# A retention layer with a mish feed-forward: the order of states and y in the opening, two conversions on GpSimd, and identity matmuls of 32 columns

## The chip, the core and the metric

The kernel runs on one core of a Trainium2 chip. The core has TensorE (PE in the profile; its weight loads are listed as PEld), VectorE (DVE), ScalarE (ACT), GpSimd (POOL) and SyncE (SP), which issues the loads and stores. The metric is the device time in microseconds of one execution of the program.

## The reference

Two steps. First a recurrent retention over 4 batches, 8 heads, 768 positions and a head dimension of 64; then a feed-forward layer on the 3,072 rows that come out, with 512 inputs, 2,048 hidden columns and the activation mish, h · tanh(softplus(h)).

```python
for t in range(S):
    state = gamma[None, :, None, None] * state + np.einsum('bhd,bhe->bhde', k[:, :, t], v[:, :, t])
    y[:, :, t] = scale * np.einsum('bhd,bhde->bhe', q[:, :, t], state)
...
h = x @ w_in
sp = np.where(h > 20.0, h, np.log1p(np.exp(np.minimum(h, 20.0))))
g = h * np.tanh(sp)
return (g @ w_out).astype(np.float32)
```

## The kernel before

The recurrence is computed in chunks of 128 positions, six to a batch, 24 in all. For a chunk, TensorE forms the *scores* k·q, VectorE multiplies them by a mask (and converts them to 16 bits), TensorE multiplies the masked scores with v (the *present* part of y) and the incoming state with q (the *past* part). The *outer* products of k and v, summed over the chunk, renew the state. The powers of gamma are put into q, k and v when they are converted from 32 to 16 bits, so that a state only has to be multiplied once every two chunks (by the table gch).

The work is cut into blocks: the first has four chunks, ten more have two. For each block the kernel forms y, turned so that it can be the input of the feed-forward (tile xt), then h = x·w_in with mish (tile g), then g·w_out. Later blocks replace eight block products by seven, with sums of quarter matrices (wsum, gsum, tmat) made on VectorE. All instructions are written in the order in which each engine runs them; every engine takes its own in that order, and the waits between engines follow from the tiles. PSUM tiles come from pools of a few banks (mmps with 3, atps with 2, pxps with 1); a new tile waits until the readers of the one that had its bank before are done.

The change lies nearly all in `first_block`, the opening. It treats the first four chunks as two *pairs*, 0 and 1. The steps, with the lines that the profile names:

- `load_first_q`, `load_pair` (L254, L298): SyncE loads q of the first four chunks, then k of both pairs in halves, then v of both pairs in halves, then the weights of the first matrix in pieces (L200, tile wi).
- `cast_first_q`, `cast_pair` (L279, L315, L319): conversion of q on VectorE, of pair 0's k on VectorE, of pair 1's k on GpSimd, of all four halves of v on ScalarE (L315: a plain multiplication by a constant).
- `spin` (L477): matmuls of the identity into a scratch bank whose result nobody reads.
- `turn_first_q`, `turn_pair` (L266, then a copy on ScalarE, L270): turning q and k on TensorE by a matmul with the identity.
- `pair_scores` (L349 and the mask on VectorE, L357, which writes am for pair 0 and a part of wsum for pair 1), called for each half of each pair.
- `pair_outer` (L370), into u; `pair_state` (L381 to L388) makes from it, in turn, the states named mid (after the first chunk of a pair: a copy on ScalarE for pair 0, an addition on VectorE for pair 1) and sth (after the second chunk: on VectorE an addition into suh and a multiplication).
- `pair_present` (L398) in two halves of 16 matmuls, the second marked own; `pair_past` (L408), 8 matmuls; both add up in y for pair 0 and in z for pair 1. Between the two halves of present a tiny copy named seen reads one column of y (ScalarE, L1350) or of z (VectorE, L1357); the second half waits for it.
- `pair_xt` (L425): ScalarE copies y and z into xt. The first h matmuls, `open_in` (L699), read xt and the weights that `cast_win` (L224) converts on GpSimd and VectorE; `next_in` (L727) and `g1` (L744) go on with h, one *unit* of 128 hidden columns after another.

GpSimd also writes the mask tables: keep_four, tri_half and keep_two. Only keep_four is used in the opening.

`IN_HALVES` names units of h whose matmuls of 512 columns are written as two of 256.

Of the kernel before, what the change touches and what calls it, by code (L numbers as in the profile page):

```python
# [12 lines left out]
ALU = mybir.AluOpType  # L13
# [3 lines left out]
def kernel(  # L17
# [91 lines left out]
    for h in range(H):  # L109
        p0 = h // 2 % 2 * D  # L110
        nc.gpsimd.memset(
            gch[p0:p0 + D, h // 4 * 2 + h % 2], float(gamma[h] ** (2 * C)))
    seen = cpool.tile([P, 1], FP32, name="seen")
# [14 lines left out]
    IN_HALVES = {0: range(NFB - 7, NFB), 1: range(NFB - 4, NFB), 2: range(NFB)}  # L128
# [171 lines left out]
    def cast_pair(n, nm, a, scales=None, on=None):  # L300
# [13 lines left out]
        if scales is None:  # L314
            nc.scalar.mul(dst, src, BOOST)  # L315
        else:
            by = scale_by_head(scales[:, mine]) if nm != "v" else scales[:, mine].unsqueeze(
                3).broadcast_to((P, H // 2, 2, D))
            (on or nc.gpsimd).tensor_tensor(dst, src, by, op=ALU.mult)  # L319
# [151 lines left out]
    def spin(n, per=HP, to=None):  # L471
        if to is None:
            to = pairs[min(x for x in pairs if type(x) is tuple and x[1] == "at")]
            to = to.rearrange("p h i r c -> p h (i r) c")
        for i in range(0, n, per):
            m = min(per, n - i)
            nc.tensor.matmul(  # L477
                to[:, 0, :m], ident, ident.unsqueeze(1).broadcast_to((P, m, P)),
                start=True, stop=True)

# [10 lines left out]
    def half(n):  # L491
        return slice(n * D, (n + 1) * D)
# [797 lines left out]
    def first_block():  # L1290
# [17 lines left out]
        nc.gpsimd.memset(tri_half, 0.0)  # L1308
        for n in range(2):
            nc.gpsimd.affine_select(  # L1310
                out=tri_half[half(n)], in_=tri_half[half(n)], compare_op=ALU.is_gt, fill=1.0,
                base=0, pattern=[[-1, 2], [-2, D // 2]], channel_multiplier=1)
        keep_from(keep_two, 2, [[1, 2], [-1, 2], [-2, D]])
        spin(38, 1)
        spin(2, 2)
# [12 lines left out]
        spin(8)  # L1328
        pair_scores(0, 1)
        turn_pair(1, "k", 0, True)  # L1330
        cast_pair(0, "v", 0)
        turn_pair(1, "k", 1, True)
        cast_pair(0, "v", 1)
        cast_pair(1, "v", 0)
        pair_at(1, 0)
# [13 lines left out]
        spin(6, to=aside)  # L1349
        nc.scalar.copy(seen, y[1][:, 1, 0, :1])  # L1350
        cast_pair(1, "v", 1)
        pair_present(0, y, True)
        pair_past(0, y, 1)
        pair_state(0, u, 1)
# [3 lines left out]
        u = u_next  # L1358
        for a in range(2):
            pair_outer(1, u, a)  # L1360
        for m in range(2):
            pair_xt(0, y, m)
        pair_state(1, u, 0)
# [276 lines left out]
```

## Time and profile before

| | |
|---|---|
| median of 3 runs | 190.93 us (190.66 to 191.94) |
| the profiled execution | 190.69 us |
| its span in the trace | 188.9 us |
| TensorE busy | 183.6 us (97%) |
| VectorE, ScalarE, GpSimd busy | 142.9, 111.5, 65.3 us |
| mean granted TensorE clock | 1.0 of full speed |

The span runs from the program's first instruction to its last; the execution's own time is 1.8 us longer. Times in the rows are counted from the start of the span. A busy TensorE in a row means that matmuls follow one another without a gap; the end of a matmul is modelled and includes its way through the array, so that neighbours overlap in the rows and the distance of their starts is what one costs.

### The profile page before, as it was taken

The page shows a single profiled execution, that of the slowest core. Times are in us where ns is not written, and L with a number is a line of the kernel's source. Part 1 is how long each engine was busy: PE and PEld are TensorE (multiplying, and loading weights), DVE is VectorE, ACT ScalarE, POOL GpSimd, SP SyncE. Part 2 cuts the span into 40 slices and gives each one's busy share as a digit, 9 for nine tenths or more (in the row PEclk, how much of TensorE's full clock was granted, in tenths as well). Part 3 has the DMA queues.
Part 4 walks back from the last instruction along what each step waited for, and adds up shares of the span by engine and source line. Part 5 has one row for each costly group of instructions (what it writes and reads, how often), then busy time and mean ns, then how long its engine had stood idle before and what let it go on. Part 6 is the DMA issues. An engine that isn't in the chain of part 4 may idle for free.

```text
span 188.9 us, 7938 instructions
## 1 busy us (share of the span) xinstructions
PE 183.6 (97%) x3438; PEld 163.6 (87%) x3438; DVE 142.9 (76%) x310; ACT 111.5 (59%) x213; POOL 65.3 (35%) x93
## 2 busy tenths in 40 slices
PE   7999999999999999999999999999999999999993
PEld 7756478888898998998998998998998998988983
DVE  0888679885977967887898597687698698666862
ACT  3575767264646554793684584683673773874651
POOL 5072000578509246331354614714534800000000
PEclk9999999999999999999999999999999999999999
DMA  5999999999999899999999886993999980301103
GB/s 166 308 312 388 386 385 367 298 325 219 192 240 307 177 209 238 208 205 233 214 197 261 209 169 148 188 225 85 220 173 240 218 162 5 115 3 51 64 0 116
DMA packets 83235, 38.84 MB, mean 206 GB/s; under 512 B 58240, under 2 KB 76288, under 8 KB 83200
## 3 DMA queue, kind: packets, MB, share of 16 engines
q1 hardware_dynamic: 82912, 38.22, 85.8%
q8 instruction: 27, 0.44, 1.0%
q10 hardware_dynamic: 288, 0.11, 0.2%
q14 instruction: 8, 0.07, 0.1%
HBM read 27.31 MB, written 6.29 MB: 178 GB/s over the span
## 4 chain that ended last, share of the span: by engine, by line
PE 92%; DMA 3%; SPq 1%; POOL 1%; issue 1%; ACT 0%; DVE 0%; POOLq 0%; DVEq 0%
PE h_ps L957 27%; PE o_ps L1179 23%; PE h_ps L744 12%; PE o_ps L1073 10%; PE o_ps L801 7%; DMA kf<-in_k_dram 3%; PE y_ps L620 3%; PE h_ps L699 2%; PE u_ps L514 1%; PE at L506 1%; PE y_ps L398 1%; POOL qk L319 1%; PE h_ps L727 1%; PE t_ps L266 1%; PE at L349 1%
## 5 line engine op out<-in xcount | busy, mean ns | idle before, releaser
L957 PE MATMUL h_ps<-xt,wsum 128*128 128x128 f16 x512 | 33.5, 219 | 0.0
L969 ACT ACTIVATE g<-h_ps 128x512 f16<-128x512 f32 x48 | 27.5, 598 | 6.6 <-PE h_ps L957 6.6
L957 PEld LDWEIGHTS <-wsum 128*128 128x128 f16 x512 | 29.9, 98 | 0.0
L957 PE MATMUL h_ps<-xt,win 128*128 128x128 f16 x384 | 28.0, 219 | 0.0
L957 PEld LDWEIGHTS <-win 128*128 128x128 f16 x384 | 23.6, 98 | 0.3
L1179 PEld LDWEIGHTS <-gsum 128*128 128x128 f16 x232 | 21.5, 98 | 2.6
L744 PE MATMUL h_ps<-xt,win 128*128 128x128 f16 (+2 forms) x276 | 23.7, 246 | 0.0
L744 PEld LDWEIGHTS <-win 128*128 128x128 f16 x276 | 20.4, 98 | 3.0
L753 ACT ACTIVATE g<-h_ps 128x512 f16<-128x512 f32 x26 | 15.5, 597 | 10.2 <-PE h_ps L744 10.2
L1179 PE MATMUL o_ps<-tmat,gsum 128*128 128x256 f16 (+1 forms) x176 | 21.5, 268 | 0.0
L458 POOL TENSOR_TENSOR v<-vf,qvs 128x512 f16<-128x512 f32 x18 | 18.9, 1067 | 6.1 <-DMA vf<-in_v_dram 6.1
L439 POOL TENSOR_TENSOR qk<-qf,qvs 128x512 f16<-128x512 f32 x18 | 18.7, 1041 | 1.3 <-PE y_ps L398 1.3
L1021 DVE TENSOR_TENSOR h_ps<-h_ps,hsum 128x512 f32<-128x512 f32 x16 | 11.1, 695 | 10.2 <-PE h_ps L957 10.1
L1179 PEld LDWEIGHTS <-g 128*128 128x128 f16 x184 | 16.5, 98 | 1.6
L1000 ACT COPY h_ps<-h_ps 128x512 f32<-128x512 f32 x16 | 9.3, 584 | 12.6 <-issue 8.7
L678 ACT CAST xt<-y_ps 128x512 f16<-128x512 f32 x16 | 10.8, 738 | 8.6 <-PE y_ps L620 8.6
L1189 ACT COPY snap<-o_ps 128x256 f32<-128x256 f32 (+1 forms) x22 | 8.2, 373 | 11.0 <-PE o_ps L1179 11.0
L1179 PE MATMUL o_ps<-wout,g 128*128 128x256 f16 (+1 forms) x120 | 14.5, 265 | 0.0
L453 POOL TENSOR_TENSOR qk<-kf,qvs 128x512 f16<-128x512 f32 x12 | 12.5, 1043 | 4.6 <-DMA kf<-in_k_dram 4.6
L1538 POOL COPY summed<-gsum 128x1 f16<-128x1 f16 x7 | 1.6, 234 | 36.1 <-DVE gsum L918 28.7
L801 PEld LDWEIGHTS <-g 128*128 128x128 f16 x120 | 11.4, 98 | 1.7 <-DVE tmat L895 0.2
L1202 DVE TENSOR_TENSOR osb<-o_ps,snap 128x256 f32<-128x256 f32 (+1 forms) x22 | 9.1, 414 | 4.3 <-ACT snap L1189 2.8
(128 smaller groups left out, 343.9 us busy)
## 6 DMA issues: line engine op xcount, KB each, us to landing
out_dram<-osb SPq DMA_DIRECT2D x22, 256.0 KB, 4.0
qf<-in_q_dram SPq DMA_DIRECT2D x18, 256.0 KB, 5.0
kf<-in_k_dram SPq DMA_DIRECT2D x14, 256.0 KB, 5.6
vf<-in_v_dram SPq DMA_DIRECT2D x14, 256.0 KB, 5.5
wt<-in_moe_w_out_dram SPq DMA_DIRECT2D x6, 512.0 KB, 8.7
vf<-in_v_dram SPq DMA_DIRECT2D x20, 128.0 KB, 3.9
wi<-in_moe_w_in_dram SPq DMA_DIRECT2D x4, 512.0 KB, 8.7
kf<-in_k_dram SPq DMA_DIRECT2D x16, 128.0 KB, 4.1
```

The lines of the kernel that those rows point to most:

```text
L439: nc.gpsimd.tensor_tensor(in_place(q16.rearrange("p (w x) d -> p w x d", x=2)), by_head(qf), scale_by_head(qs_two[:, heads]), op=ALU.mult)
L453: nc.gpsimd.tensor_tensor(dst, src, boosts.rearrange("p (w y) -> p w y", y=2).unsqueeze(3).broadcast_to((P, H // 2, 2, D)), op=ALU.mult)
L458: nc.gpsimd.tensor_tensor(cast[g][2], loaded.pop(g)[2], vs[g % 2].unsqueeze(2).broadcast_to((P, H, D)), op=ALU.mult)
L678: nc.scalar.copy(dst[:, :, x], src)
L744: nc.tensor.matmul(h_ps[:, j, cols], wins[s][f // 2][:, bp, f % 2 * P:(f % 2 + 1) * P], xts[blk][:, bp, cols], start=(bp == 0 and at == 0) ...
L753: nc.scalar.activation(gt, h_ps, AF.Mish, scale=inv_boost3)
L801: nc.tensor.matmul(banks[ij][:, t], x(f)[:, t * P:(t + 1) * P], w(f), start=ij in open_banks, stop=f == fs[-1], skip_group_check=True)
L957: nc.tensor.matmul(o_ps[:, f], w(f // 2, k)[:, f % 2 * P:(f % 2 + 1) * P], x[:, k], start=begin and f == 0 and k == 0, stop=k == 1, skip_g ...
L969: nc.scalar.activation(gt[:, f:f + n, j * C:(j + 1) * C], src, AF.Mish, scale=inv_boost3)
L1021: nc.vector.tensor_tensor(pf[p], pa[p], m5[p], op=ALU.add)
L1073: nc.tensor.matmul(o_ps[:, cols], x(f), w(f)[:, cols], start=first and z == 0, stop=z == n - 1, skip_group_check=True)
L1179: nc.tensor.matmul(o_ps[:, c:c + wide], x(f), w(f)[:, c:c + wide], start=first and f == 0 and c == cols.start, stop=f == n - 1, skip_group ...
```

## The change

The states of both pairs are now made before the second half of pair 0's present and before pair 1's y. Two of the four v halves are converted on GpSimd. The tables tri_half and keep_two are written at the program's beginning. Ahead of the first turn stand 16 identity matmuls of 32 columns and 34 of 128, in place of 38 of 128 and one of 256; six later identity turns (one matmul of 512 and one of 256) are gone, and one of two 512 wide ones behind the first turn of k. Pair 1's first k turn moves ahead of pair 0's second scores. Units 9 and 10 of the first block are written whole.

```diff
+    nc.gpsimd.memset(tri_half, 0.0)
+    for n in range(2):
+        nc.gpsimd.affine_select(
+            out=tri_half[n * D:(n + 1) * D], in_=tri_half[n * D:(n + 1) * D],
+            compare_op=ALU.is_gt, fill=1.0, base=0, pattern=[[-1, 2], [-2, D // 2]],
+            channel_multiplier=1)
+    keep_from(keep_two, 2, [[1, 2], [-1, 2], [-2, D]])
     seen = cpool.tile([P, 1], FP32, name="seen")
...
-    IN_HALVES = {0: range(NFB - 7, NFB), 1: range(NFB - 4, NFB), 2: range(NFB)}
+    IN_HALVES = {0: range(NFB - 5, NFB), 1: range(NFB - 4, NFB), 2: range(NFB)}
...
-        if scales is None:
+        if scales is None and on is not None:
+            on.tensor_tensor(
+                dst, src, boosts[:, mine].unsqueeze(2).unsqueeze(3).broadcast_to(
+                    (P, H // 2, 2, D)), op=ALU.mult)
+        elif scales is None:
             nc.scalar.mul(dst, src, BOOST)
...
+    def spin_small(n):
+        to = pairs[min(x for x in pairs if type(x) is tuple and x[1] == "at")]
+        for _ in range(n):
+            nc.tensor.matmul(
+                to[:, 0, 0, 0, :D // 2], ident, ident[:, :D // 2], start=True, stop=True)
...
             cast_pair(1, "k", a, vs_two)
-        nc.gpsimd.memset(tri_half, 0.0)
-        for n in range(2):
-            nc.gpsimd.affine_select(
-                out=tri_half[half(n)], in_=tri_half[half(n)], compare_op=ALU.is_gt, fill=1.0,
-                base=0, pattern=[[-1, 2], [-2, D // 2]], channel_multiplier=1)
-        keep_from(keep_two, 2, [[1, 2], [-1, 2], [-2, D]])
-        spin(38, 1)
-        spin(2, 2)
+        spin_small(16)
+        spin(34, 1)
         turn_first_q(0, 0)
...
         turn_pair(0, "k", 1, True)
-        spin(8)
+        spin(4)
+        turn_pair(1, "k", 0, True)
         pair_scores(0, 1)
-        turn_pair(1, "k", 0, True)
         cast_pair(0, "v", 0)
         turn_pair(1, "k", 1, True)
-        cast_pair(0, "v", 1)
+        cast_pair(0, "v", 1, None, nc.gpsimd)
         cast_pair(1, "v", 0)
+        cast_pair(1, "v", 1, None, nc.gpsimd)
         pair_at(1, 0)
...
         pair_present(0, y, False)
         aside, u_next = u_banks()
-        spin(6, to=aside)
         nc.scalar.copy(seen, y[1][:, 1, 0, :1])
-        cast_pair(1, "v", 1)
+        pair_state(0, u, 1)
+        u = u_next
+        for a in range(2):
+            pair_outer(1, u, a)
+        pair_state(1, u, 0)
         pair_present(0, y, True)
-        pair_past(0, y, 1)
-        pair_state(0, u, 1)
         z = [mmps.tile([P, 2, 2, C], FP32, name="y_ps", tag="mm") for _ in range(2)]
         pair_present(1, z, False)
         nc.vector.tensor_copy(seen, z[1][:, 1, 0, :1])
-        u = u_next
-        for a in range(2):
-            pair_outer(1, u, a)
+        pair_past(0, y, 1)
         for m in range(2):
             pair_xt(0, y, m)
-        pair_state(1, u, 0)
         pair_present(1, z, True)
         for m in range(2):
             pair_past(1, z, m)
```

VectorE's order around the opening's states, before (am and wsum are the masked scores of pairs 0 and 1, suh, sth and mid the states, win the converted weights):

```order
L357 TENSOR_TENSOR wsum_385<-at,keep_four 128x1024 x2
L386 TENSOR_TENSOR suh<-u_ps,mid 128x256
L388 TENSOR_TENSOR sth<-suh,gch 128x256
L1357 COPY seen<-y_ps 128x1
L383 TENSOR_TENSOR mid<-u_ps,sth 128x256
L224 COPY win_582<-wi 128x512 x2
```

and now, at the same place:

```order
L368 TENSOR_TENSOR wsum_397<-at,keep_four 128x1024 x2
L397 TENSOR_TENSOR suh<-u_ps,mid 128x256
L399 TENSOR_TENSOR sth<-suh,gch 128x256
L394 TENSOR_TENSOR mid<-u_ps,sth 128x256
L1370 COPY seen<-y_ps 128x1
L231 COPY win_590<-wi 128x512 x2
```

The addition that makes mid of pair 1 and the tiny copy have changed places; nothing else on VectorE has.

GpSimd's order from the table gch to the first weights, before (qk_190 is pair 1's converted k):

```order
L111 MEMSET gch 64x64 x8
L319 TENSOR_TENSOR qk_190<-kf,qvs 128x2x4x64 x2
L1308 MEMSET tri_half 128x64
L1310 AFFINE_SELECT tri_half<-tri_half 64x64 x2
L102 MEMSET keep_two 128x256
L104 AFFINE_SELECT keep_two<-keep_two 64x256 x2
L224 COPY win_582<-wi 128x512 x2
```

and now (v_369 and v_373 are the second halves of v of pairs 0 and 1):

```order
L111 MEMSET gch 64x64 x8
L113 MEMSET tri_half 128x64
L115 AFFINE_SELECT tri_half<-tri_half 64x64 x2
L102 MEMSET keep_two 128x256
L104 AFFINE_SELECT keep_two<-keep_two 64x256 x2
L330 TENSOR_TENSOR qk_204<-kf,qvs 128x2x4x64 x2
L322 TENSOR_TENSOR v_369<-vf,qvs 128x4x2x64
L322 TENSOR_TENSOR v_373<-vf,qvs 128x4x2x64
L231 COPY win_590<-wi 128x512 x2
```

The tables stand ahead of the k conversions, and two v conversions behind them.

TensorE, where pair 0's first half of present ends (its last matmul has v_359), before:

```order
L398 MATMUL y_ps<-am,v_359 64x128
L477 LDWEIGHTS ident
L477 MATMUL u_ps<-ident 128x512
L477 LDWEIGHTS ident
L477 MATMUL u_ps<-ident 128x256
L398 LDWEIGHTS v_351
L398 MATMUL y_ps<-am,v_351 64x128
```

and now:

```order
L409 MATMUL y_ps<-am,v_369 64x128
L409 LDWEIGHTS v_369
L409 MATMUL y_ps<-am,v_369 64x128
L381 LDWEIGHTS qk_204
L381 MATMUL u_ps<-v_371,qk_204 64x64
```

Two identity matmuls and the own half of present stood there; now pair 1's outer products follow at once, 32 of them, ahead of that half. TensorE's list has 6,878 rows in both versions, a weight load and a matmul counted as one row each.

## The prediction

> **What bounds the kernel now.** I read the span first, then the busy time by stretches, then the chain in order of time for the opening, where nearly all of the change lies.
>
> ```profile
> span 188.9 us, 7938 instructions
> ```
>
> ```profile
> 9.00:17.00 8.00, 7.14 (x237) 4.51 (x238) 6.74 (x11) 5.86 (x14) 4.36 (x9) 1.00 1.11 338
> 17.00:185.00 168.00, 168.00 (x3111) 151.58 (x3110) 131.61 (x292) 101.62 (x194) 58.17 (x67) 1.00 0.87 200
> ```
>
> The first figure after the comma is TensorE's busy time: 7.14 of 8.00 in the opening, and from 17 us on it never stops (168.00 of 168.00). Whatever the change does before 17 us therefore arrives undiminished at the end, and nothing later can amplify it. The question is only when the first h matmul starts.
>
> ```profile
> 10.21 1.05 POOL qk L319
> ...
> 14.42 0.34 PE y_ps L398 x13
> 14.76 0.40 issue
> 15.16 0.25 PE y_ps L398 x3
> ...
> 15.85 0.17 DVE seen L1357
> ...
> 16.06 0.42 PE y_ps L398 x16
> ...
> 16.86 3.58 PE h_ps L699 x24
> 20.44 1.73 PE h_ps L727 x8
> 22.17 8.70 PE h_ps L744 x68
> ```
>
> The opening's chain, in order of time: the last k conversion on GpSimd (which waits for its load), turns, scores and y on TensorE, a stall of 0.40 us called "issue", a tiny VectorE copy ("seen") for which the last present matmuls wait, then h. The timeline has the first h matmul at 16.79:
>
> ```profile
> 16.28 0.31 PE L408 MATMUL y_ps<-qkt,sth 64*64 64x128 f16 x8
> 16.55 0.31 PE L408 MATMUL y_ps<-qkt,mid 64*64 64x128 f16 x8
> 16.79 0.72 PE L699 MATMUL h_ps<-xt,win 128*128 128x256 f16 x5
> ```
>
> VectorE, which feeds this, in the same view:
>
> ```profile
> 12.53 2.36 DVE L357 TENSOR_TENSOR wsum<-at,keep_four 128x1024 f16<-128x1024 f32 x2 [0.34 <-PE at L349]
> 14.80 0.41 DVE L386 TENSOR_TENSOR suh<-u_ps,mid 128x256 f32<-128x256 f32 x1
> 15.32 0.42 DVE L388 TENSOR_TENSOR sth<-suh,gch 128x256 f16<-128x256 f32 x1
> 15.85 0.16 DVE L1357 COPY seen<-y_ps 128x1 f32<-128x1 f32 x1
> 16.07 0.42 DVE L383 TENSOR_TENSOR mid<-u_ps,sth 128x256 f16<-128x256 f32 x1
> ```
>
> It is packed from 12.53: two masks, then state, copy, state. And the other two helpers:
>
> ```profile
> 14.12 0.65 ACT L315 ACTIVATE v<-vf 128x512 f16<-128x512 f32 x1
> 15.56 1.07 ACT L425 CAST xt<-y_ps 128x512 f16<-128x512 f32 x2 [0.79 <-PE y_ps L408]
> 16.89 1.07 ACT L425 CAST xt<-y_ps 128x512 f16<-128x512 f32 x2 [0.26 <-PE y_ps L408]
> 9.20 2.04 POOL L319 TENSOR_TENSOR qk<-kf,qvs 128x512 f16<-128x512 f32 x2 [5.55 <-DMA kf<-in_k_dram]
> 15.63 0.61 POOL L224 CAST win<-wi 128x512 f16<-128x512 f32 x1 [2.37 <-DMA wi<-in_moe_w_in_dram]
> ```
>
> **The stall of 0.40 us** waits for no semaphore. It lies ahead of the 14th of 16 matmuls, which is row 448 of TensorE's list in the program's order. Instructions come by a DMA queue of their own:
>
> ```profile
> q8 instruction: 27, 0.44, 1.0%
> ```
>
> The same rows asked for the 0.05 us from 12.70, then from 18.90, each with one packet that begins there:
>
> ```profile
> q8 instruction: 1, 0.02, 149.1%
> ...
> q8 instruction: 1, 0.02, 130.6%
> ```
>
> The share is that of 16 engines in 0.05 us, so the packets took 1.19 and 1.05 us. And what ran around row 192:
>
> ```profile
> 9.07 0.42 PE L349 MATMUL at<-qkt 64*64 64x128 f16 x16
> 9.42 0.40 PE L266 MATMUL t_ps<-ident,qk 128*128 128x128 f16 x4
> ```
>
> 27 packets for 6,878 rows is one per 256 rows, and 448 = 192 + 256. The reading that fits: when TensorE passes row 192 + 256n it asks for the block that begins 256 rows further on. It passed row 192 at 9.42 (the first turn matmul); the packet began at 12.7, behind the load queue; row 448 ran at 15.16. That is 5.7 us from asking to having, 1.25 of them behind the packet's end. Here it cost almost nothing: what followed waited anyway for VectorE's state addition, which ended at 14.80 + 0.41 = 15.21, because z takes over u's banks.
>
> The Trainium skill ("Runtime: NRT & Kernel Launch", section "Instruction fetch mechanics") gives TensorE 2,048 instructions of store, blocks of 256, and calls fetching mostly hidden. By that the stall would be absent; the trace agrees on the 256 alone. The sum below, with no stall, would come out the same, as VectorE sets it.
>
> **The change, part by part.**
>
> *States ahead of y* is the part that counts. VectorE's order becomes suh, sth, mid, seen instead of suh, sth, seen, mid. The copy and sth kept their 0.11 us distance (15.32 + 0.42 to 15.85), so mid starts at 15.85 at the earliest and runs 0.42 to 16.27; seen starts about 0.07 before that ends (as the following cast did) and ends at 16.36. The last present matmuls follow it by 0.05 (15.85 + 0.16 to 16.06): they start at 16.41, 0.35 later than before. Part comes back: before, the 8 last past matmuls waited for mid (16.07 + 0.42, start 16.55); now mid is long there. Present 16.06 to 16.28 is 0.22, the sth half of past about 0.11, the mid half with the change of shape 16.55 to 16.79, 0.24. Sum 0.57, so h starts at 16.41 + 0.57 = 16.98 against 16.79: **+0.19 us**.
>
> Does TensorE reach that point in time? Its outer products of the second pair want a bank that the first mask frees (12.53 + 1.2 = 13.7), which is no later than they come. Then it sits at row 448 again, now in the middle of the outer products of the second pair, with nothing to do instead since the six identity matmuls are gone. It passes row 192 up to 0.3 earlier (inside the first scores, from 9.07, not in the turn at 9.42), so the block is there between 14.9 and 15.16. Behind it stand 27 outer products, 32 present and 8 past matmuls:
>
> ```profile
> 15.31 0.43 PE L398 MATMUL y_ps<-wsum,v 64*64 64x128 f16 x16
> 15.53 0.46 PE L370 MATMUL u_ps<-v,qk 64*64 64x64 f16 x32
> ```
>
> Start to start, 16 present take 0.22 and 32 outer some 0.28: together 0.25 + 0.45 + 0.1, so z is done by 15.7 to 15.9 and the past of the first pair by 15.7 to 16.0. Seen, at 16.20, is not held up. ScalarE's copies to xt move from 15.56 to about 16.2 at the latest (0.25 behind the past, as in the rows above): first two to 17.27, next two then start at 17.2 against 16.89, their first done at 17.8. The second eight h matmuls want it at 16.98 + 0.87 = 17.85 (1.73 / 8 is 0.216 for 512 columns, 0.108 for 256, eight times). Zero to 0.1 us.
>
> *Two v conversions on GpSimd.* Adding rows of the same form: 2.04 / 2 = 1.02 us against 0.63 on ScalarE. The last v load is issued at 7.9 and lands some 5.6 later, at 13.5:
>
> ```profile
> L298 SPq DMA_DIRECT2D vf<-in_v_dram x4: 782/958/1235, 4.9 to 7.9; - x4
> DMA to landing us min/median/max: 5.5/5.6/5.9
> ```
>
> So the second one ends at about 14.7, as ScalarE's did (14.12 + 0.65 = 14.77). The block of instructions and VectorE's 15.21 hide it; without them it would cost at most what it is later than ScalarE's start of use, some 0.4. GpSimd's next task, the weight cast at 15.63, waits for its load and keeps its time. The first starts after the k conversions and ends before 13; what TensorE gains by it falls into the row-448 stall: nothing.
>
> *Masks first.* They ran between the k conversions' end (9.20 + 2.04 = 11.24) and the wait for weights (15.63 - 2.37 = 13.26), so 2.0 us, and now lie in GpSimd's idle 5.55 us ahead of 9.20: nothing. At the worst they slow VectorE's first q conversions beside them, which the cover named next takes too.
>
> *Identity matmuls.* 16 narrow and 34 wide replace 38 and one double.
>
> ```profile
> 1.36 4.45 PE L477 MATMUL at<-ident 128*128 128x128 f16 x39 [1.36 <-POOL ident L97]
> 5.66 0.61 PE L266 MATMUL t_ps<-ident,qk 128*128 128x128 f16 x4
> 8.00 0.40 PE L266 MATMUL t_ps<-ident,qk 128*128 128x128 f16 x4
> ```
>
> 4.45 / 39 gives about 0.107 start to start. A narrow one costs between a quarter of it (0.027, if columns count) and all of it (0.107, if the weight load counts): the run to the first turn is 4.1 to 5.35 us, against the 4.3 from 1.36 to 5.66. I take the lower half, as in these rows the load of weights lies beside the matmul; the upper end delays the first turn by 1.0 us, of which VectorE's 0.34 us wait ahead of 12.53 and its waits for q and k eat nearly all, leaving 0.1.
>
> *One turn ahead of the scores, four columns fewer of spin:* a turn of 0.22 us fills the wait for ScalarE's copy; the next scores move by less than 0.05. *Units 9 and 10 of h no longer halved:* four whole matmuls take 1.73 / 2 = 0.865, and ten units, seven of them halved, took 8.70; so a halved one takes (8.70 - 3 x 0.865) / 7 = 0.872, and two give -0.01. With them TensorE's list keeps its length.
>
> **Sum:** +0.19, +0.05 for xt, -0.01: +0.2 us. The profiled execution took 190.69 (span 188.9 and 1.8 around it), so 190.9. The median of the runs shown is 190.93, 0.24 higher; on that it is 191.1. I name 191.0.
>
> **Rivals.** *The second block is late.* This is the one that ends slower. Row 704 stands six wide matmuls after the start of the second weight slice (now) instead of fourteen: from 16.79 + 3.48 + 13 x 0.216 = 23.1 it moves to 16.98 + 3.48 + 5 x 0.216 = 21.5. Its block is asked for at row 448, about 15.1. The packet began at 18.9, 3.75 us after asking at 15.16, took 1.05, and the first block was usable 1.25 after its packet, so 21.2. From 0.3 us more on, TensorE stalls one for one; 1 us more gives +0.7: 191.6. Loads fill the queues in both versions, which speaks for it; the estimate leaves a margin, which speaks against. 0.18.
>
> *VectorE's chain moves up.*
>
> ```profile
> 11.54 0.59 PE L477 MATMUL at<-ident 128*128 128x512 f16 x2
> 12.06 0.42 PE L349 MATMUL at<-qkt 64*64 64x128 f16 x16
> ...
> 12.06 0.26 PEld L349 LDWEIGHTS <-qkt 64*64 64x64 f16 x16 [0.42 <-ACT qkt L270]
> ```
>
> The second pair's scores are put down to a wait of 0.42 us for ScalarE's turn copy, which now comes earlier. If that wait was real and not the tail of the identity matmuls (11.54 + 2 x 0.216 = 11.97, then a change of shape), masks and states come up to 0.4 earlier and the sum is +0.19 - 0.4 = -0.2: 190.6. The floor is the weight cast, 15.63 + 0.61 = 16.24, -0.5: 190.2. 0.2.
>
> *Narrow matmuls leave the clock low.* The turns show it: 0.61 us for four at 5.66, 0.40 at 8.00. If full speed came one such stretch later, near 10, four turns and scores would take 0.2 more each, with 0.34 of cover: +0.4, 191.3. 0.08. The Trainium skill ("TensorE: Matmul & The Clock Gate", Part 1 on the clock gate) ties full speed to a busy stretch of about 3.4 us in a free-running window; by it the 34 wide ones alone fill the stretch and the time stays.
>
> *Nothing moves* beyond the scatter of the runs (190.66 to 191.94): 0.09. The forecast has 0.45.
>
> **Range and chances.** The fast end is the floor 190.2; the slow end is the late block on the median's base, 191.9. One per cent is 1.9 us, about what a measurement of this kernel can tell from no change. No case reaches it faster (the floor is -0.5); slower takes the late block and a cold clock together. Faster 0.015, within 0.955, slower 0.03.
>
> **What would show it.** VectorE: mid at about 15.85, seen at about 16.2, the copy after it; the first h matmul at about 17.0; an "issue" stall of 0.8 to 1.3 us on TensorE inside the outer products of the second pair, ending at 14.9 to 15.2; GpSimd's v conversions ending near 12.9 and 14.7; no gap on TensorE near 21.5. I am wrong if h starts ahead of 16.7 or after 17.4, if row 704 stalls, or if anything after 30 us differs in length.

## The result and the profile after

The changed kernel takes 193.88 us, the median of six executions (192.38 to 195.17), against 190.99 (190.66 to 191.94, six) before: 1.0137 times as long, with a 95% interval of 1.0098 to 1.0175. The forecast was 191.0, within 190.2 to 191.9. The profiled execution took 194.97 us. The ratios, here and below, leave out executions over 1.5% above the fastest of their kernel, so that a ratio can be lower than the medians suggest.

From the page of the changed kernel, its span; then the busy times in the same two stretches as before (TensorE first behind the comma):

```profile
span 193.2 us, 7937 instructions
```

```profile
9.00:17.00 8.00, 5.42 (x201) 3.57 (x201) 6.76 (x8) 3.86 (x9) 4.88 (x5) 1.00 1.11 339
17.00:185.00 168.00, 165.91 (x3101) 148.11 (x3098) 131.82 (x291) 101.42 (x193) 58.50 (x67) 1.00 0.91 199
```

The opening keeps TensorE busy for 5.42 of 8.00 us, where it was 7.14. And behind 17 us, where before not a gap was left, 2.09 us are idle. Both have to be explained.

The chain of waits in the opening, in order of time (start, length, what):

```profile
7.90 7.08 DMA vf<-in_v_dram
...
15.04 1.05 POOL v L322
...
16.14 0.32 PE u_ps L381 x16
16.45 0.45 PE y_ps L409 x32
16.90 0.16 PE y_ps L419 x8
17.07 1.06 ACT xt L436 x2
...
18.17 3.52 PE h_ps L716 x23
21.69 1.73 PE h_ps L744 x8
```

It runs through a load that the chain before did not have: the last quarter of v, issued at 7.9 us as before, lands at 14.98 instead of 13.5. Everything waits for it in turn: GpSimd's conversion, pair 1's outer products, present and past of pair 0, ScalarE's copies, h. The second group of h matmuls starts at 21.69 instead of 20.44, 1.25 us late.

TensorE's rows of the same stretch, then VectorE's and GpSimd's:

```profile
13.80 0.24 PE L381 MATMUL u_ps<-v,qk 64*64 64x64 f16 x5 [0.19 <-DVE wsum L368]
14.65 0.28 PE L381 MATMUL u_ps<-v,qk 64*64 64x64 f16 x11 [0.60 <-issue]
16.14 0.32 PE L381 MATMUL u_ps<-v,qk 64*64 64x64 f16 x16 [1.20 <-POOL v L322]
...
17.82 0.28 PE L716 MATMUL h_ps<-xt,win 128*128 128x256 f16 x1
```

```profile
15.32 1.05 DVE L399 TENSOR_TENSOR sth<-suh,gch 128x256 f16<-128x256 f32 x1
16.51 0.42 DVE L394 TENSOR_TENSOR mid<-u_ps,sth 128x256 f16<-128x256 f32 x1
17.03 0.16 DVE L1370 COPY seen<-y_ps 128x1 f32<-128x1 f32 x1
```

```profile
15.04 1.04 POOL L322 TENSOR_TENSOR v<-vf,qvs 128x512 f16<-128x512 f32 x1 [2.20 <-DMA vf<-in_v_dram]
```

Three things are new: GpSimd waits 2.20 us for the load; VectorE's sth takes 1.05 us beside that conversion instead of 0.42; and TensorE, which had 0.40 us of idle here, now has 0.60 of "issue" and 1.20 of waiting for v. The long sth is not on the chain: it ends at 16.37, and mid waits for the last of the outer products, which end at 16.46.

**Why the load is late.** The view of the tile vf has the time from issue to landing of the four v loads; the transfers between 11.95 and 12.00 us show the instruction packet, which began at 12.72 before:

```profile
L305 SPq DMA_DIRECT2D vf<-in_v_dram x4: 782/956/1230, 4.9 to 7.9; - x4
...
DMA to landing us min/median/max: 5.5/5.7/7.1
```

```profile
q8 instruction: 1, 0.02, 147.6%
```

A load is spread over 16 DMA engines, and the trace has 16 semaphore records for it. By these, 15 parts of the last v load were in at 13.16 to 13.47 us, as before (13.16 to 13.48 for all 16); the sixteenth came at 14.98. The 11 matmuls that were added in front move row 192 from the turn (9.42 us) into the scores ahead of it (9.16). The asking for an instruction block leaves no row in the trace; "asked for" is here, by the prediction's reading, the time at which TensorE passes row 192. So it asked 0.26 us earlier, and the packet began 0.77 us earlier. It took 1.18 us, and one part of the load is 1.5 us late. This account by the instruction block is what the experiments test first; the rival to it is that the order of the work, or GpSimd itself, makes v late.

### The profile page after: what moved, and what is told of

Read it like the earlier page. It is cut to its first block, busy times and chain, and to the rows that moved or that the text cites. A ratio compares the mean times of both kernels' runs of the same rounds, so it can differ in the third digit from the quotient of the medians.

```text
span 193.2 us, 7937 instructions
## 1 busy us (share of the span) xinstructions
PE 183.1 (95%) x3438; PEld 162.0 (84%) x3438; DVE 145.4 (75%) x310; ACT 110.6 (57%) x211; POOL 68.8 (36%) x95
## 4 chain that ended last, share of the span: by engine, by line
PE 78%; DVE 7%; DMA 7%; SPq 4%; ACT 1%; issue 1%; POOL 1%; ACTq 0%
PE h_ps L974 25%; PE o_ps L1196 23%; PE h_ps L761 10%; PE o_ps L1090 7%; PE o_ps L818 4%; DMA vf<-in_v_dram 4%; SPq L305 3%; DMA kf<-in_k_dram 3%; PE y_ps L637 3%; PE h_ps L716 2%; PE u_ps L531 1%; DVE wout L243 1%; PE at L523 1%; PE h_ps L744 1%; DVE gsum L926 1%
## 5 line engine op out<-in xcount | busy, mean ns | idle before, releaser
L974 PEld LDWEIGHTS <-win 128*128 128x128 f16 x384 | 23.6, 98 | 0.8 <-issue 0.5
L761 PEld LDWEIGHTS <-win 128*128 128x128 f16 x268 | 19.7, 98 | 3.7
```

The source lines that it names most:

```text
L761: nc.tensor.matmul(h_ps[:, j, cols], wins[s][f // 2][:, bp, f % 2 * P:(f % 2 + 1) * P], xts[blk][:, bp, cols], start=(bp == 0 and at == 0) ...
L974: nc.tensor.matmul(o_ps[:, f], w(f // 2, k)[:, f % 2 * P:(f % 2 + 1) * P], x[:, k], start=begin and f == 0 and k == 0, stop=k == 1, skip_g ...
```

## The experiments

Ten kernels ran, in three sittings, each beside the kernel before on the same chip. The expectations name their theories by letters; what was found is told in words, since the letters differ between sittings. "Half clock" counts executions whose mean granted clock was 0.991 or less; the kernel before had none in the 64 of these sittings. "Landed" is the last v load.

| run | median us (before) | ratio, 95% interval | block asked for, packet | landed | first h | half clock |
|---|---|---|---|---|---|---|
| kernel before | 190.99 | 1 | 9.42, 12.72 | 13.48 | 16.79 | 0 of 64 |
| changed | 193.88 (190.99) | 1.0137 [1.0098, 1.0175] | 9.16, 11.95 | 14.98 | 17.82 | 3 of 6 |
| e1 rows back | 192.35 (191.34) | 1.0032 [0.9991, 1.0073] | 9.42, 12.78 | 13.50 | 17.21 | 1 of 10 |
| e2 identity alone | 191.97 (191.34) | 1.0030 [0.9996, 1.0065] | 9.13, 11.98 | 14.99 | 17.07 | 0 of 10 |
| e3 v on ScalarE | 193.75 (191.34) | 1.0051 [1.0005, 1.0097] | 9.13, 11.88 | 14.84 | 17.23 | 5 of 10 |
| e4 order alone | 191.54 (191.34) | 1.0012 [0.9987, 1.0037] | 9.47, 12.75 | 13.59 | 17.13 | 0 of 10 |
| e5 changed again | 194.58 (191.47) | 1.0141 [1.0087, 1.0194] | 9.20, 11.93 | 14.94 | 18.41 | 4 of 4 |
| e6 idle filled | 192.89 (191.47) | 1.0086 [1.0053, 1.0119] | 9.26, 11.83 | 14.84 | 17.68 | 0 of 10 |
| e7 old order | 193.79 (191.47) | 1.0070 [1.0025, 1.0115] | 9.10, 11.95 | 14.97 | 17.77 | 6 of 10 |
| e8 three of the changes | 191.20 (191.47) | 0.9989 [0.9958, 1.0020] | 9.44, 12.79 | 13.51 | 17.07 | 0 of 10 |
| e9 collision | 192.25 (191.43) | 1.0059 [1.0039, 1.0080] | 10.31, 13.56 | 14.37 | 18.16 | 0 of 4 |
| e10 ScalarE, filled | 192.19 (191.43) | 1.0046 [1.0022, 1.0069] | 9.72, 11.98 | 14.99 | 17.83 | 0 of 5 |

The v loads of e9 and e10 were issued some 0.9 and 0.6 us later than the others' in the profiled execution (the last one at 8.80 and 8.50, before at 7.92); their times are compared as distances. The intervals of e1, e2, e4 and e8 include 1: by their medians these four cannot be told from the kernel before, and what is said of them rests on the rows of one profiled execution each.

### e1: the instruction block at its old time

The 11 additional matmuls are still there, but behind row 192:

```diff
-        spin_small(16)
-        spin(34, 1)
+        spin(38, 1)
+        spin(2, 2)
...
         turn_pair(0, "k", 1, True)
+        spin_small(11)
         spin(4)
```

> The change, but with the identity matmuls of the kernel before ahead of the first turn (38 of 128 columns, one of 256) and 11 of the narrow ones put behind the second k turn of pair 0, so that TensorE's row 192 is again that turn's first matmul while the list keeps its 6,878 rows. Theory F (the instruction block is asked for earlier, its packet takes one load engine ahead of the last v load): the last v load lands at about 13.5 us again instead of 14.98, the last v conversion on GpSimd ends near 14.7 instead of 16.09, VectorE's sth takes 0.42 us instead of 1.05, the first h matmul stands near 17.0; median 191.0 to 191.4, granted clock 1.0 in all runs. Theory G (the conversion on GpSimd and the collision beside VectorE are late by themselves): the last conversion still ends near 16, h near 17.8, median 193 to 194. Theory O (the order of the states alone): as the change, 193 to 194.

GpSimd, VectorE and TensorE in this kernel:

```profile
13.57 1.04 POOL L322 TENSOR_TENSOR v<-vf,qvs 128x512 f16<-128x512 f32 x1 [0.72 <-DMA vf<-in_v_dram]
```

```profile
15.32 0.43 DVE L399 TENSOR_TENSOR sth<-suh,gch 128x256 f16<-128x256 f32 x1
15.89 0.42 DVE L394 TENSOR_TENSOR mid<-u_ps,sth 128x256 f16<-128x256 f32 x1 [0.15 <-PE u_ps L381]
16.42 0.16 DVE L1371 COPY seen<-y_ps 128x1 f32<-128x1 f32 x1
```

```profile
15.43 0.41 PE L381 MATMUL u_ps<-v,qk 64*64 64x64 f16 x27 [1.38 <-issue]
...
17.21 0.28 PE L716 MATMUL h_ps<-xt,win 128*128 128x256 f16 x1
```

Order and GpSimd are as in the changed kernel, so the rival by order or GpSimd falls and the account by the instruction block holds. With the packet at its old place, the load is in time, the conversion ends at 14.61 and nothing collides: this is the opening that was forecast, 0.2 us late in places. The first h comes 0.61 us earlier than in the changed kernel, and of the 2.9 us between the medians 1.0 are left. That is more than was expected: the median lies above 191.0 to 191.4, one execution had the lower clock, and the block was usable at 15.43 only, so that the outer products wait for it longer than the prediction's 14.9 to 15.2.

### e2, e3, e4: one part alone, and GpSimd left out

e2 is the kernel before with the identity matmuls of the change (and two more units whole); e3 is the changed kernel with all v conversions on ScalarE; e4 is the kernel before with the new order of states and y alone.

```diff
e2:
-        spin(38, 1)
-        spin(2, 2)
+        spin_small(16)
+        spin(34, 1)
...
         turn_pair(0, "k", 1, True)
-        spin(8)
+        spin(4)
...
-        spin(6, to=aside)
```

```diff
e3:
-        cast_pair(0, "v", 1, None, nc.gpsimd)
+        cast_pair(0, "v", 1)
         cast_pair(1, "v", 0)
-        cast_pair(1, "v", 1, None, nc.gpsimd)
...
         nc.scalar.copy(seen, y[1][:, 1, 0, :1])
+        cast_pair(1, "v", 1)
         pair_state(0, u, 1)
```

```diff
e4:
         cast_pair(1, "v", 1)
-        pair_present(0, y, True)
-        pair_past(0, y, 1)
         pair_state(0, u, 1)
...
+        pair_state(1, u, 0)
+        pair_present(0, y, True)
         z = [mmps.tile([P, 2, 2, C], FP32, name="y_ps", tag="mm") for _ in range(2)]
         pair_present(1, z, False)
         nc.vector.tensor_copy(seen, z[1][:, 1, 0, :1])
+        pair_past(0, y, 1)
```

> The kernel before with the identity part of the change alone: 16 narrow and 34 of 128 columns ahead of the first turn, one of two 512 wide ones left out, the six ahead of the second present left out, units 9 and 10 whole. Order, v conversions and masks as before. Theory F: the packet of the instruction block begins near 12.0 instead of 12.7, the last v load lands near 15.0 instead of 13.5, so ScalarE's last v conversion starts at 15.0 instead of 14.12 and h 0.4 to 0.9 us later than before; median 191.4 to 192.2. Theories G and O: nothing of the kind, the load lands at 13.5, median 190.7 to 191.2.

> The change with all four v conversions on ScalarE as before. Theory F: the last v load still lands near 15.0; ScalarE converts it in 0.63 us instead of 1.05 and VectorE's sth is no longer beside GpSimd (0.42 instead of 1.05), so h comes 0.4 to 0.7 us earlier than in the change, near 17.2; median 191.5 to 193. Theory G: all of the loss goes, median 190.7 to 191.2, h at 16.8. Theory O: nothing changes, 193 to 194.

> The kernel before with the order of the states and y alone (pair 0's second state, pair 1's outer products and its first state ahead of the own half of pair 0's present and of pair 1's y). Theory F: the last v load lands near 13.5, nothing is late; the h matmuls start 0.1 to 0.3 us later than before, as mid now stands ahead of seen on VectorE; median 191.0 to 191.4. Theory O: most of the loss is here, median 192.5 or more. Theory G: as before, 190.7 to 191.2.

e2 settles from the other side what moves the load: nothing is changed but identity matmuls, and it lands at 14.99. ScalarE then converts from 15.02, and h is 0.28 late, less than the 0.4 to 0.9 expected:

```profile
15.02 0.63 ACT L315 ACTIVATE v<-vf 128x512 f16<-128x512 f32 x1 [0.80 <-DMA vf<-in_v_dram]
...
17.07 0.61 PE L705 MATMUL h_ps<-xt,win 128*128 128x256 f16 x4
```

e4, without them, has it at 13.6, and gives the price of the order by itself:

```profile
15.90 0.42 DVE L383 TENSOR_TENSOR mid<-u_ps,sth 128x256 f16<-128x256 f32 x1
16.34 0.16 DVE L1360 COPY seen<-y_ps 128x1 f32<-128x1 f32 x1
```

```profile
17.48 3.52 PE h_ps L699 x23
21.00 1.73 PE h_ps L727 x8
```

The first h is 0.34 us late (17.13), the second group of h 0.56 (21.00 against 20.44), because h now also waits for ScalarE's copies: 0.34 instead of the 0.19 of the sum, and 0.22 instead of 0.05 for xt. Not all of this is the order. The masks of this execution begin 0.05 us later (12.58), and its block, whose packet begins at 12.75, is usable at 15.42 where the kernel before had it at 15.16; the copies to xt hang on it. By the medians e4 is 0.2 us slower, which its interval does not tell from nothing.

e3 has the late load and no collision, since ScalarE does the conversion:

```profile
15.27 0.43 DVE L399 TENSOR_TENSOR sth<-suh,gch 128x256 f16<-128x256 f32 x1
```

Its first h is at 17.23, 0.59 ahead of the changed kernel's. The start of the second group of h, in the chain of e1 and then of e3:

```profile
21.07 1.73 PE h_ps L744 x8
```

```profile
21.11 1.73 PE h_ps L744 x8
```

e1 has the order and no late load, e3 the order and the late load, the changed kernel (21.69) both and GpSimd. e1's outer products wait for the block until 15.43, e3's for v until 15.55, so that the late load behind the new order makes a difference of 0.04 us only. The changed kernel is 0.58 us behind e3, and by as much its last v is ready later: at 16.09, on GpSimd (1.05 us behind a load at 14.98), and in e3 at 15.51, on ScalarE (0.63 us behind a load at 14.84). The collision beside sth adds nothing, as mid follows the outer products by 0.05 us in both (16.46 to 16.51, 15.87 to 15.92).

But half of its executions lost something else: five had a mean clock of 0.991 and took 193.9 to 195.9 us, and of the five at full clock three took 191.1 to 191.9. The other two took 193.5 and 193.6; why stays open. So the median, 193.75, missed the 191.5 to 193 of the theory by the instruction block and is where the theory by the order had it, while the rows are as the first described them.

### e5, e6, e7: the clock

The changed kernel once more; the changed kernel with TensorE's idle at 14 us filled; and the changed kernel with the old order.

```diff
e6:
-    IN_HALVES = {0: range(NFB - 5, NFB), 1: range(NFB - 4, NFB), 2: range(NFB)}
+    IN_HALVES = {0: range(NFB - 4, NFB), 1: range(NFB - 4, NFB), 2: range(NFB)}
...
         pair_state(0, u, 1)
+        spin(16, to=aside)
         u = u_next
```

```diff
e7:
-        pair_state(0, u, 1)
-        u = u_next
-        for a in range(2):
-            pair_outer(1, u, a)
-        pair_state(1, u, 0)
         pair_present(0, y, True)
+        pair_past(0, y, 1)
+        pair_state(0, u, 1)
...
-        pair_past(0, y, 1)
+        u = u_next
+        for a in range(2):
+            pair_outer(1, u, a)
...
+        pair_state(1, u, 0)
```

> The changed kernel, nothing edited, as the control for the other three. Theory I (the instruction block that TensorE asks for at 9.16 us instead of 9.42 is fetched ahead of the last packets of the last v load): that load lands at 14.8 to 15.0 us, the last GpSimd v conversion runs to 16.0 to 16.2, the mask on sth beside it takes about 1.05 us instead of 0.42, first h matmul at 17.7 to 17.9; 192.4 to 195 us. Rival J (the late load was a chance of the one profiled execution): the load lands at 13.5 again, first h at about 17.1 and 191.2 to 191.8. Rival K (the larger part of the loss sits in the fourth batch of columns, after 83 us): the opening is as in J, and TensorE still waits a microsecond after 83 us.

> The changed kernel with four identity matmuls of 512 columns put in front of the second pair's outer products, where TensorE idles from about 13.8 to 14.7 us (and one more unit of the first block done whole). Theory L (the idle of the opening, some 2 us with little work in it, costs a window of the clock in some executions, 1.7 us each): first h as in the changed kernel, 17.7 to 17.9, but the executions with a mean clock of 0.991 go (none or one of ten, where the changed kernel had three of six), and the median falls by 0.7 to 1.3 us to about 192.4. Rival M (those executions have another cause): their share stays, and the median stays within 0.4 us of the changed kernel's.

> The changed kernel with states and y in the order of the kernel before; narrow identity matmuls, two v conversions on GpSimd and masks first stay. Theory I: v load at 14.8 to 15.0, GpSimd conversion to about 16.1, the mask on sth slowed to about 1 us beside it, first h at 17.3 to 17.6: 192.0 to 192.8. Rival N (the order of the program is what makes the GpSimd conversion late, the instruction block only follows it): load lands at 13.5, first h at about 16.9, 191.0 to 191.3.

e5 shows the opening of the first profile again (I, against J and K): load at 14.94, conversion beside sth (0.96 us). Its profile also caught what the first one had not, a stretch at half the clock, so that its first h, at 18.41, lies above the 17.7 to 17.9 expected. Busy times of e5 in stretches of 3.41 us, laid so that they meet the changes of the granted clock in the trace (TensorE first; the granted clock is the third figure from the end):

```profile
9.69:13.11 3.42, 2.89 (x80) 1.61 (x80) 2.95 (x3) 2.59 (x5) 2.65 (x3) 1.00 1.17 298
13.11:16.52 3.41, 1.50 (x101) 1.12 (x93) 3.16 (x5) 0.65 (x3) 1.51 (x2) 1.00 1.05 383
16.52:19.94 3.42, 3.30 (x75) 2.52 (x64) 2.73 (x8) 2.15 (x4) 1.07 (x2) 0.50 1.05 386
```

The same of e7, of the first profile of the changed kernel and of e1, then of e6 in the emptiest 3.41 us of its opening, wherever they begin:

```profile
13.12:16.53 3.41, 1.90 (x112) 1.35 (x101) 3.13 (x4) 1.70 (x5) 1.50 (x2) 1.00 1.05 384
16.53:19.94 3.41, 3.36 (x63) 2.49 (x52) 2.77 (x8) 1.07 (x2) 0.92 (x2) 0.50 1.05 386
```

```profile
11.78:15.19 3.41, 2.37 (x99) 1.44 (x98) 3.20 (x4) 1.61 (x5) 1.19 (x2) 1.00 1.10 354
15.19:18.60 3.41, 2.17 (x93) 1.74 (x93) 3.03 (x8) 1.55 (x4) 2.26 (x3) 1.00 1.06 389
```

```profile
12.94:16.35 3.41, 1.84 (x120) 1.51 (x121) 3.12 (x5) 0.79 (x3) 1.65 (x2) 1.00 1.03 377
16.35:19.76 3.41, 3.12 (x55) 2.34 (x51) 2.82 (x7) 2.05 (x4) 0.61 (x1) 1.00 1.05 387
```

```profile
13.69:17.10 3.41, 2.19 (x80) 1.35 (x77) 3.06 (x7) 0.52 (x3) 1.79 (x2) 1.00 1.05 386
```

In e5 and e7 a stretch in which TensorE was busy for 1.50 or 1.90 us of 3.41 is followed by one at half the clock; in the changed kernel's first profile 2.17 and 2.37 are not. But neither is the 1.84 of e1, so busy time alone does not decide. What orders these five is the columns of the stretch's matmuls, each times the share of the array that its weights fill (a quarter for 64 by 64): 1,952 in e5 and 2,368 in e7 with half the clock behind them, 2,816 and 4,096 in the changed kernel and 2,848 in e1 without. At the program's end 2,816 had half the clock behind them too (e9), so that a line, if there is one, lies near that. This was counted afterwards, and no run was made to test it. Where the stretches begin differs from execution to execution, so the same kernel pays in some and not in others. The kernels divide by the emptiest 3.41 us of the opening in their profile: with at least 2.19 us busy, no execution of 49 (e2, e4, e6, e8, e9, e10) and none of the kernel before had the lower clock; with less than 1.9 (the changed kernel twice, e1, e3, e7) 19 of 40 had. e1, whose emptiest 3.41 us have 1.6 us, paid in one of ten only. The price is read best in e7, which had both: 193.94 us is the median of its six at the lower clock, 192.14 that of its four others, 1.8 us apart, about half a stretch.

e6 keeps the late load, the collision and the first h (17.68), and only fills the idle: none of ten at the lower clock, and the median falls by 1.7 us from e5's to 192.89 (by 1.0 from 193.88), to a little above the 192.4 expected. Theory L stands, M falls. The Trainium skill ("TensorE: Matmul & The Clock Gate", Part 1) describes a free-running window of 3,413 ns and half speed after an idle window; the traces agree on the length and on a start that differs between executions, but here windows that were 44% (e5) and 56% (e7) busy were followed by half speed.

e7 keeps the load late (14.97) with the old order, which speaks for I against N; its 17.77 for the first h lies above the 17.3 to 17.6 expected, and part of it is the half clock from 16.53 on. Its median, too, lies above the 192.0 to 192.8, as six of ten had the lower clock.

### e8: three of the changes

The kernel before with masks first, pair 1's k turn ahead of the scores, and one v conversion on GpSimd, with row 192 kept at its time (one identity matmul of 32 columns stands there in place of one of 512).

```diff
-        spin(8)
-        pair_scores(0, 1)
+        spin_small(1)
+        spin(4)
         turn_pair(1, "k", 0, True)
+        pair_scores(0, 1)
...
-        cast_pair(0, "v", 1)
+        cast_pair(0, "v", 1, None, nc.gpsimd)
```

> The kernel before with three of the changes only: masks built first on GpSimd, the second pair's k turn ahead of the first pair's scores (one identity matmul of 64 columns and four of 512 less there, so that row 192 and its time stay as before), and the second v conversion alone on GpSimd. Theory I: block asked for at 9.4, v load lands at 13.5, last v conversion ends at 14.2 instead of 14.8, first h between 16.6 and 16.8, 190.8 to 191.2 us where the kernel before has 191.0. Rival O (moving a v conversion to GpSimd is itself the cost, wherever the load lands): VectorE's masks are slowed beside it and first h is at 17.0 or later, 191.3 to 191.8.

```profile
15.44 0.25 PE L409 MATMUL y_ps<-am,v 64*64 64x128 f16 x3 [0.79 <-issue]
...
17.07 0.61 PE L716 MATMUL h_ps<-xt,win 128*128 128x256 f16 x4
```

The last v is converted 0.32 us earlier than before (ScalarE, to 14.45), and nothing is gained: TensorE waits for its instruction block until 15.44, where the kernel before had it at 15.16, and h follows that. No different from the kernel before (0.9989 [0.9958, 1.0020]). Neither theory had named this bound: the first h is where O put it, the time at the upper edge of the 190.8 to 191.2 that I has, and sth was not slowed (0.43 us). The best version found is thus no faster than the kernel before.

### e9, e10: the collision alone, and the sum

e9 is the kernel before with one more conversion on GpSimd, held back until 15 us, whose result nothing reads. e10 is e3 with e6's filling.

```diff
e9:
         cast_pair(1, "v", 1)
+        beside = castp.tile([P, 2, H // 2, D], FP16, name="v16", bufs=7)
+        nc.scalar.copy(beside[:, 0, 0, :1], pairs[1, "v", 1][:, 0, 0, :1])
+        nc.gpsimd.tensor_tensor(
+            beside.rearrange("p r h d -> p h r d"), pairs[1]["v"][1],
+            boosts[:, H // 2:].unsqueeze(2).unsqueeze(3).broadcast_to((P, H // 2, 2, D)),
+            op=ALU.mult)
```

> The kernel before, with one GpSimd conversion added that nothing uses: v of the second pair's second half once more, into a spare tile, held back until ScalarE's own conversion of it is done (14.8 us). Nothing else moves: v load at 13.5, instruction block at 15.2 as before. Theory P (a GpSimd operation of this size slows the VectorE mask on sth beside it, whatever else happens): GpSimd runs from about 15.0 to 16.1, sth takes 1.0 us instead of 0.43, and the copy seen, mid and the first h matmul come 0.5 to 0.6 later, first h at about 17.3 to 17.4: 191.5 to 191.9 us where the kernel before has 191.0. Rival Q (sth took 1.05 us in the changed kernel for another reason, such as the order of the states): sth stays at 0.43, first h within 0.15 us of 16.79, 190.9 to 191.3.

> The changed kernel with all v conversions on ScalarE, and the four identity matmuls of 512 columns in TensorE's idle at 14 us (one more unit whole). It takes away the collision and the idle, and leaves the late load and the order. Theories I and L together: v load at 14.8 to 15.0, sth 0.43, first h at 17.1 to 17.3, no execution with a mean clock of 0.991, 191.4 to 192.0 us. Rival R (narrow identity matmuls or masks first cost something that no run so far has shown): the median stays above 192.5, or executions at 0.991 remain.

GpSimd and VectorE in e9, then in e10:

```profile
16.02 1.04 POOL L1354 TENSOR_TENSOR v<-vf,qvs 128x512 f16<-128x512 f32 x1 [1.87 <-ACT v L1353]
...
16.21 1.13 DVE L388 TENSOR_TENSOR sth<-suh,gch 128x256 f16<-128x256 f32 x1
```

```profile
15.72 0.61 POOL L231 CAST win<-wi 128x512 f16<-128x512 f32 x1 [3.91 <-DMA wi<-in_moe_w_in_dram]
...
15.88 0.73 DVE L399 TENSOR_TENSOR sth<-suh,gch 128x256 f16<-128x256 f32 x1
```

Where a GpSimd operation was under way when sth began, sth ended 0.28 us after that operation: 16.36 and 16.08 in the changed kernel, 17.34 and 17.06 in e9, 16.61 and 16.33 in e10. GpSimd's operation kept its 1.04 and 0.61 us. So VectorE waits for the other to end. The weight cast that GpSimd begins right behind, at 16.03 in the changed kernel and 17.00 in e9, took 0.81 us instead of 0.61; whether it waited for sth in its turn was not tested. From the last v conversion's end to the first h matmul e9 needs 18.16 - 15.66 = 2.50 us against 16.79 - 14.77 = 2.02: where sth is waited for, as here, the collision costs 0.48, a little under the 0.5 to 0.6 expected; P stands, Q falls. The ratio, 1.0059, is 1.1 us, and the median, 192.25, lies above the 191.5 to 191.9; what makes the rest stays open. The Trainium skill ("SBUF — State Buffer", section "Who interferes with whom") has the rule: a VectorE instruction with two SBUF inputs contends with a GpSimd instruction that reads SBUF, and the order of issue decides which of the two blocks. The traces agree, down to the mask and state additions that read PSUM, which kept their 1.2 and 0.42 us beside GpSimd.

e10 has no execution at the lower clock, and 192.19 us against the 193.75 of e3. It missed its 191.4 to 192.0 a little: its sth took 0.73 us, as the weight cast now lay beside it. The v load, issued 0.6 us later than in the kernel before, landed in the expected 14.8 to 15.0 by chance. R, which wanted more than 192.5, falls.

## Why the prediction was wrong

**The step that failed first** is the one on the v conversions: "The last v load is issued at 7.9 and lands some 5.6 later, at 13.5", so that the second conversion "ends at about 14.7". It ended at 16.09. Just ahead of that the prediction had that row 192 is passed "up to 0.3 earlier" and that the block arrives earlier for it. It did (14.65), but the packet that brings it is a transfer beside those of v: whenever it came early, one of the 16 parts of the v load was late (e2 with nothing else changed, e1 with the packet back at its old time and v in time). The one number was moved and the other, which depends on it, was read from the trace of before. The cover that was named for the conversion, VectorE's 15.21, was gone with it.

**No price was named for what a GpSimd operation does to VectorE beside it.** A row of the profile before would have given one: VectorE's second sth took 0.80 us beside a GpSimd weight cast.

```profile
17.68 0.80 DVE L388 TENSOR_TENSOR sth<-suh,gch 128x256 f16<-128x256 f32 x1
```

In the changed kernel this happened to cost nothing of its own: sth was done at 16.37, and mid had to wait until 16.46 for the outer products, which the late v held up. Where sth is waited for, as in e9, it costs 0.48. So a shift of 0.26 us of one request became 1.5 us of one load, and behind that load a conversion of 1.05 us on GpSimd, where ScalarE takes 0.63, held up all that follows.

**"Whatever the change does before 17 us therefore arrives undiminished at the end, and nothing later can amplify it"** was wrong twice. The clock: the emptier opening costs 1.8 us more in the executions in which a stretch falls badly, seven of ten of the changed kernel; with the idle filled none of ten paid (e6). The rival that named the clock sought it in the narrow matmuls and gave it 0.08; these behaved as taken, 16 in 1.81 - 1.36 = 0.45 us, 0.028 each, and the first turn came at 5.62. It lay in the waits for the block and for v, in which nothing was left to do. And behind 17 us: work that was hidden under a busy TensorE does not stay hidden when its input moves. Between 29 and 40 us, where TensorE had no gap before, it idled 0.18 us in the changed kernel and 0.56 in e5, waiting for VectorE, whose conversions of the second weights and sums make up the chain there. In the profiled execution a further 1.6 us went between 83 and 100 us. The two stretches in the changed kernel, and the waits of the second:

```profile
29.00:40.00 11.00, 10.82 (x106) 9.53 (x104) 10.27 (x13) 5.13 (x10) 3.12 (x4) 1.00 1.09 333
83.00:100.00 17.00, 15.39 (x359) 13.72 (x357) 13.63 (x28) 9.68 (x20) 6.29 (x8) 1.00 0.90 180
```

```profile
POOL v L469 <- DMA vf<-in_v_dram: 6.5, 1, 6.5
...
PE h_ps L974 <- ACT h_ps L1017: 1.0, 1, 1.0
```

GpSimd waited for a v load till 85.31 and then ran beside VectorE's gsum, two SBUF inputs again, which took 1.25 and 1.15 us where it otherwise takes 0.42. e5 lost only 0.2 us there and e6, e7, e9 nothing, so it is not part of the usual loss; what made the load late in that execution stays open.

**Term by term.** *States ahead of y*: right in mechanism, 0.34 for 0.19 (e4), of which 0.05 is that execution's later start. mid began at 15.90 against 15.85; seen came 0.02 behind mid, not 0.07 ahead of its end, and later by 0.14. *xt*: 0.22 for 0.05 (e4), with the block usable at 15.42 and not between 14.9 and 15.16. *Masks first*: nothing, as far as e8 shows, which has them with two other parts. *Identity matmuls*: their own price held (0.107 for one of 128 columns is 4.3 / 40; the 4.45 / 39 of the prediction would be 0.114), their place in the list was the loss. *The second block late*, the rival with 0.18: row 704 did not stall, the row there has its usual distance; the fetch was asked for at 14.65 and the packet began at 18.50. *VectorE's chain moves up*: it did not, wsum began at 12.53 in both. Of the signs of being wrong that were named, two came: h after 17.4 (17.82), and gaps after 30 us.

**The sum as it turned out.** Of the 2.9 us between the medians the opening makes 1.25, by the chains of waits of the two profiled executions. With the load in time, e1 has 0.63 of it and e4 0.56, for the order and for a block that was usable 0.26 to 0.27 us later than in the profile of the kernel before; how much of this each makes was not separated. The other 0.6 come with the late load and GpSimd's conversion of it. The lower clock adds 1.8 in most executions; e6, which takes only this away, is at 192.89. What is left, from case to case, are the later gaps. The parts do not add: the late load alone, in the old order and converted by ScalarE, moves the first h by 0.28 us (e2), and behind the new order it hides (e3).

## What to carry to other kernels

An instruction fetch is a transfer like any other. When a change adds or takes away rows ahead of a point where a block is asked for, look up which load is then on the way, and who waits for it; the load's time from the old trace no longer holds. Idle time that a change opens up on TensorE can be paid twice, here when it filled about half of a stretch of 3.41 us: keep filler matmuls where waits grow, and look at the granted clock of several executions, not of one. And before work is given to GpSimd, look for VectorE instructions with two SBUF inputs beside it, and whether anything waits for them.

## What was unexpected of the hardware

- A quarter of a microsecond decided over the load. Counted from the issue of the last v load, the block was asked for 1.49 to 1.51 us behind it in the kernel before, e1, e4, e8 and e9; the packet began 4.8 to 4.9 us behind it, and the load took 5.6. In the seven others it was asked for 1.22 to 1.27 us behind it; the packet began 3.5 to 4.1 us behind it, and the load took 6.5 to 7.1. Nothing lies between. In the changed kernel one packet of 16 KB, 1.2 us long, came with a sixteenth of a load of 256 KB that was 1.5 us late, and the whole load with it.
- From the packet's end to the first instruction of the block 1.25 to 1.5 us passed (13.91 to 15.16 before, 13.13 to 14.65 changed, 13.97 to 15.43 in e1).
- The clock fell for a stretch of 3.41 us after one that was 44% (e5) or 56% (e7) busy, and did not after one of 64% (changed kernel) or of 54% (e1). Counted in columns times the filled share of the array, these openings fall in order: 1,952 and 2,368 against 2,816 and 2,848.
- sth ended 0.28 us behind the GpSimd operation beside it, in every trace in which it was slowed, whether by a v conversion or by a weight cast.
